# Starting expert weights a step earlier and reordering the handover from attention to experts

## The chip, the cores and the metric

The kernel runs on one core of a Trainium2 chip. The time is that of the device for one execution, in microseconds, as a median of timed runs. A profile of one execution is a separate run with its own span; positions in it are counted from the span's start. The engines are called PE (TensorE), DVE (VectorE), ACT (ScalarE), POOL (GpSimd) and SP (SyncE). A line number such as L446 is a line of the kernel before.

## The reference, cut to what matters

Two layers follow each other. The first is a gated linear attention (an mLSTM cell) over 4 batches of 8 heads, 768 steps and head size 40; its output, put together over the heads, gives 3072 rows of 320. The second is a mixture of 8 experts: a row goes to the one expert with the largest logit, through two matrices with a relu between, and is scaled by the softmax weight of that expert.

```python
def _attn_ref(q, k, v, i_gate, f_gate, o_gate):
    ...
    for t in range(S):
        m_new = np.maximum(f_gate[:, :, t] + m, i_gate[:, :, t])
        f_stab = np.exp(f_gate[:, :, t] + m - m_new)
        i_stab = np.exp(i_gate[:, :, t] - m_new)
        C = f_stab[..., None, None] * C + i_stab[..., None, None] * np.einsum('bhd,bhe->bhde', vt, kt)
        n = f_stab[..., None] * n + i_stab[..., None] * kt
        h_tilde = np.einsum('bhde,bhe->bhd', C, qt)
        denom = np.maximum(np.abs(nq), 1.0)          # nq = n . q
        y[:, :, t] = o * h_tilde / denom             # o = sigmoid(o_gate)

def _moe_ref(x, w_gate, w1, w2):
    logits = x @ w_gate
    expert_idx = np.argmax(logits, axis=1)
    ...
    for e in range(E):
        h = np.maximum(x_sorted[lo:hi] @ w1[e], 0.0)
        y_sorted[lo:hi] = h @ w2[e]
    return gate_w[:, None] * y_sorted[inv_perm]
```

## The kernel before

The attention runs in chunks of 128 rows, 24 in all, six to a batch. A loop over steps works on several chunks at once: step `s` makes the scores of chunk s+1, the transposes of s+2, the attention output of s, and the routing of older ones. Chunks are routed in teams of two: `logits`, `choose` (which expert), `gate` (softmax weight), `rank` and `place` (at which place of the expert's list). `keep_rows` scales the rows into bf16 and `send` scatters them on POOL into a sorted list in HBM. Each expert's list is then read back in tiles: tile (e, 0) has the first 256 places and holds only rows of chunks 0 to 15, tile (e, 1) the next 128. What is left over goes into extra tiles, whose weights are copied within SBUF once they are all there.

Each engine runs its instructions in the order in which they stand in the program, so that the place of a call in the source decides what it waits behind.

The weights of an expert are brought in by two functions. Both are DMAs that POOL issues[...]:

```python
    def weights_in(e, n=1):            # w1: three DMAs, 512 KB and twice 64 KB
        nc.gpsimd.dma_start(w1_all[:, e, : FL * F]..., bass.AP(moe_w1.tensor, ...))        # L181
        for i in range(2):
            nc.gpsimd.dma_start(w1_all[64 * i : 64 * i + 64, e, FL * F :], moe_w1[...])    # L186

    def weights_out(e0, n):            # w2: one DMA, 640 KB
        nc.gpsimd.dma_start(w2_all[:, e]..., moe_w2[e]...)                                 # L193
```

A tile is turned (transposed on PE, copied by DVE), goes through the first layer in pieces `u`, whose relu is DVE's for even and ACT's for odd pieces, and through the second layer, whose result ACT copies and POOL scatters to the output:

```python
    def turn(g):
        g["xT"] = spot("xT", [128, NP, n * 128], BF16)
        tp = spot("tp", [128, NP, n * 128], BF16)
        ... nc.tensor.transpose(tp[...], src[:, j, d0 : d0 + 128], ident_b[:])             # L242
        nc.vector.tensor_copy(g["xT"], tp)                                                 # L243

    def layer1(g, u):
        if u == 0: ...            # four banks "hp", the first matmuls of all pieces       # L260
        ... nc.tensor.matmul(hp[:, i, :], lhsT=w[...], rhs=xT[:, db, :], ...)              # L269
        if a == 0: nc.vector.tensor_relu(dst, hp)                                          # L275
        else:      nc.scalar.activation(dst, hp, AF.Relu)                                  # L277

    def layer2(g, j):
        zp = spot(g.get("zp", "zp"), [128, Dm], F32)
        ... nc.tensor.matmul(zp, lhsT=g["h"][...], rhs=g["w"][1][:, fb, :], ...)           # L282
        nc.scalar.copy(zo, zp)                                                             # L287
        nc.gpsimd.indirect_dma_start(out=out[:, :], ...)                                   # L289
        if j + 1 < g["n"]: pause()     # a memset on POOL, L299
```

The loop of steps, cut to what the change touches (NT is 24, PE_ is 7):

```python
        for s in range(-3, NT):
            P, odd = (s - 4) // 2, s % 2
            last = s == NT - 1
            do(scores, s + 1); do(transposes, s + 2); ...; do(values, s + 2)
            if odd and s > E and sent <= (...):
                send(sent); sent += 1
            if s == NT - 5:
                weights_in(0, 1)
            ...
            do(states, s); do(load, s + 6 if s >= -1 else -1)
            if pair: rank(P, s - 1)
            if last:
                warm(5)                # filler matmuls on PE, L569
            do(xtrans, s - 1)
            do(ogate, s + 2); do(attend, s)
            ...
            do(rows, s)                # x_sb and den on DVE, then x_sb on POOL (L446)
            if odd and 0 <= (s - 3) // 2:
                logits(...); choose(...); count(...)
            if s > E and sent <= upto:
                send(sent); sent += 1
            ...
            if s == 2 * PE_ + 5:
                for e in range(E):
                    receive(e, 0)
            if s == NT - 4: weights_out(0, 1)
            if s == NT - 3: weights_in(1, 1)
            if s == NT - 2: weights_out(1, 1)
        weights_in(2, 1)
        weights_out(2, 1)
```

What stands behind the loop is the tail: the routing of the last four chunks (team P0 with chunks 20 and 21, team P0 + 1 with 22 and 23) and the first two expert tiles, in buffers of the attention. Its order is in the diff below. The eight experts' remaining tiles follow, in the order (2,0), (3,0), (0,1), (1,1), (4,0), (2,1), (5,0), (3,1), (4,1), (6,0), (5,1), (7,0), (6,1), (7,1), and five extra tiles.

Of the kernel before, what the change touches and what calls it, by code (L numbers as in the profile page):

```python
# [9 lines left out]
BF16 = mybir.dt.bfloat16  # L10
# [9 lines left out]
def kernel(  # L20
# [153 lines left out]
    s_idx = rte.tile([128, E, NJ], I32)  # L174
    rest = rte.tile([128, 512], F32)
    zo_e = rte.tile([128, 4, Dm], F32)
    xg = [(x_all[:, NE * e : NE * (e + 1), :], x_all[:, NE * E + e : NE * E + e + 1, :]) for e in range(E)]

    def weights_in(e, n=1):
# [55 lines left out]
    def turn(g):  # L235
        n = g["n"]
        src = g["xg"] if "xg" in g else xg[g["e"]][g["k"]]
        g["xT"] = spot("xT", [128, NP, n * 128], BF16)
        tp = spot("tp", [128, NP, n * 128], BF16)
        for j in range(n):  # L240
            for a, d0 in enumerate(parts):
                nc.tensor.transpose(tp[:, a, j * 128 : (j + 1) * 128], src[:, j, d0 : d0 + 128], ident_b[:])  # L242
        nc.vector.tensor_copy(g["xT"], tp)  # L243
# [65 lines left out]
    with tc.tile_pool(name="ring", bufs=1) as ring_pool, \  # L309
# [295 lines left out]
            load(i)  # L605
        for i in range(1, NV):
            pads(i)
        sent = 0
        for s in range(-3, NT):
            P, odd = (s - 4) // 2, s % 2  # L610
            last = s == NT - 1
            do(scores, s + 1)
            do(transposes, s + 2)
            if s == -3:
                masks()
            if s == -2:
                gates()
                router()
            do(values, s + 2)
            if odd and s > E and sent <= (s - 5 if s > 2 * PE_ + 4 else s - 6):  # L620
                send(sent)
                sent += 1
            if s == NT - 5:
                weights_in(0, 1)
            pair = not odd and 0 <= P
            if pair:
                gate(P)
            do(states, s)
            do(load, s + 6 if s >= -1 else -1)
            if pair:  # L630
                rank(P, s - 1)
            if last:
                warm(5)
            do(xtrans, s - 1)
            do(ogate, s + 2)
            do(attend, s)
            if pair:
                place(P)
                if P == PE_:
                    even_out(s - 1)  # L640
            if s == 2 * PE_ + 4:
                keep_rows(s - 4)
                keep_rows(s - 3)
            elif s != 2 * PE_ + 5:
# [24 lines left out]
        assert sent == NT - 4  # L669
        early = [dict(e=e, n=NE, k=0, si=0, zp="hp") for e in range(2)]  # L670
        spots.update(
            hp=[(t_, ps1) for t_ in ("sA", "sB", "tk", "tq")], tp=[("dC", ps1)],
            h=[kq[:, i].rearrange("p a h d -> p (a h d)").bitcast(BF16) for i in range(2)],
            xT=[kq[:, 2, a].rearrange("p h d -> p (h d)").bitcast(BF16) for a in range(2)],
            zo=[zo_e[:, i, :] for i in range(4)],
        )
        for g in early:
            g["w"] = (w1_all[:, g["e"], :], w2_all[:, g["e"]])
        first, second = early
# [203 lines left out]
```

## Time and profile before

| | |
|---|---|
| time before, median of 3 runs | 218.2 us (218.13 to 219.56) |
| span of the profiled run | 208.9 us |
| granted TensorE clock, mean | 0.991 |
| PE busy | 184.8 us (88%) |
| PE weight load | 153.3 us (73%) |
| DVE busy | 125.7 us (60%) |
| ACT busy | 117.0 us (56%) |
| POOL busy | 137.7 us (66%) |
| DMA moved | 44.32 MB, mean 212 GB/s |

The chain that ended last consists of PE for 64%, of POOL for 9%, of DVE for 8%, of ACT for 6% and of DMA for 3%. Busy times are sums over the whole span and say little of a single stage: the attention loop ends near 118 us, the tail reaches to about 134, and the remaining expert tiles follow. A stage is read from windows and from the chain of waits within it. A line of the chain gives the start, the length and the instruction which the rest waited for at that time. The end of a DMA instruction on POOL in the timeline is not that of the transfer.

### The profile page before, as it was taken

The numbers are of one execution on the slowest core, as the hardware profiler recorded it, in microseconds if no ns is written. First come the engines' busy times: TensorE is split into PE (matmuls) and PEld (weight loads), VectorE is DVE, ScalarE is ACT, GpSimd is POOL, SyncE is SP. The second block draws the span as 40 slices with busy tenths as digits, with TensorE's granted clock in tenths as the row PEclk, the third lists the DMA queues.
The fourth block names the chain that finished last, engine by engine and source line by source line (L and its number), as shares of the span: only waits on it lengthen the run. The fifth ranks groups of instructions, "written<-read, shape, count | busy, mean of one in ns | idle before, by whom it ended". The sixth has DMA issues, their size and how long they took to land.

```text
span 208.9 us, 5733 instructions
## 1 busy us (share of the span) xinstructions
PE 184.8 (88%) x2051; PEld 153.3 (73%) x2060; DVE 125.7 (60%) x410; ACT 117.0 (56%) x273; POOL 137.7 (66%) x238
## 2 busy tenths in 40 slices
PE   2289999999999999998999898779999999999760
PEld 1176888888999999997788676557787777777540
DVE  7855656678787877978777644256684252534310
ACT  2458765888869978798584344224343343433320
POOL 6025779437477898784999948985437568885321
PEclk9999999999999999999999999999999999999996
DMA  7999999989999999999579999899999999999930
GB/s 135 192 193 197 198 245 197 215 175 204 197 205 175 176 173 197 189 204 175 92 140 187 265 239 209 131 206 255 240 227 221 225 250 270 399 391 382 365 123 24
DMA packets 116686, 44.32 MB, mean 212 GB/s; under 512 B 102506, under 2 KB 111725, under 8 KB 116656
## 3 DMA queue, kind: packets, MB, share of 16 engines
q1 hardware_dynamic: 105456, 25.34, 58.2%
q0 software_dynamic: 10736, 18.38, 40.0%
q8 instruction: 17, 0.28, 0.5%
q10 hardware_dynamic: 464, 0.21, 0.4%
q14 instruction: 13, 0.11, 0.1%
HBM read 39.30 MB, written 9.37 MB: 233 GB/s over the span
## 4 chain that ended last, share of the span: by engine, by line
PE 64%; POOL 9%; DVE 8%; issue 8%; ACT 6%; DMA 3%; POOLq 0%; ACTq 0%; DVEq 0%
PE zp L282 10%; PE hp L269 9%; PE hp L408 7%; PE hp L476 6%; PE tk L370 5%; PE dC L416 5%; PE tq L370 4%; PE xt L453 3%; PE sA L383 3%; PE sA L388 3%; DMA w_all<-in_moe_w_dram 3%; PE hp L260 3%; POOL out_dram L289 3%; POOL x_sorted L581 2%; PE tp L242 2%
## 5 line engine op out<-in xcount | busy, mean ns | idle before, releaser
L275 DVE TENSOR_SCALAR h<-hp 128x512 bf16<-128x512 f32 x25 | 17.3, 691 | 34.8 <-PE hp L269 16.1
L277 ACT ACTIVATE h<-hp 128x512 bf16<-128x512 f32 x25 | 14.9, 597 | 26.2 <-PE hp L269 24.8
L581 POOL DMA_INDIRECT x_sorted<-x_all,slots x24 | 25.2, 1050 | 5.8 <-issue 3.9
L446 POOL TENSOR_TENSOR x_sb<-x_sb,den 128x320 f32<-128x320 f32 x23 | 16.7, 727 | 17.4 <-DVE den L444 17.2
L289 POOL DMA_INDIRECT out_dram<-zo,s_idx x20 | 19.9, 995 | 9.7 <-DMA w_all<-in_moe_w_dram 4.8
L282 PE MATMUL zp<-w_all,h 128*128 128x320 bf16 x160 | 24.0, 299 | 0.0
L282 PEld LDWEIGHTS <-h 128*128 128x128 bf16 x200 | 18.8, 98 | 6.2
L395 ACT CAST dB<-sB 128x512 bf16<-128x512 f32 x24 | 14.0, 584 | 14.0 <-PE sB L389 12.7
L269 PEld LDWEIGHTS <-w_all 128*128 128x128 bf16 x256 | 19.0, 98 | 3.8 <-issue 1.1
L408 PE MATMUL hp<-C_sb,qT 104*128 104x82 f32 x160 | 20.6, 272 | 0.0
L287 ACT COPY zo<-zp 128x320 f32<-128x320 f32 x25 | 10.6, 425 | 17.7 <-PE zp L282 16.4
L370 PE MATMUL tk<-ident,kq 128*104 128x128 f32 x96 | 16.5, 297 | 4.1 <-DMA kq<-in_k_dram 4.1
L269 PE MATMUL hp<-xT,w_all 128*128 128x128 bf16 (+1 forms) x224 | 20.1, 243 | 0.0
L408 PEld LDWEIGHTS hp<-C_sb,qT 104*128 104x128 f32 x160 | 19.4, 192 | 0.3
L455 ACT COPY xT<-xt 128x384 f32<-128x384 f32 x24 | 11.6, 482 | 13.2 <-PE xt L453 12.9
L358 POOL CAST vAb<-vA 128x328 bf16<-128x328 f32 x24 | 11.0, 458 | 11.7 <-DVE vA L356 11.7
L396 POOL TENSOR_SCALAR_AFFINE_SELECT dB<-dB 128x512 bf16<-128x512 bf16 x24 | 16.5, 689 | 2.2 <-ACT dB L395 2.0
L416 PE MATMUL dC<-vA,kq 128*104 128x82 f32 x160 | 17.8, 254 | 0.0
L476 PE MATMUL hp<-wg_sb,xT 128*128 128x8 f32 x144 | 17.7, 256 | 0.0
L393 DVE TENSOR_TENSOR dA<-sA,cmask 128x512 bf16<-128x512 f32 x24 | 16.0, 668 | 1.9 <-PE sA L388 1.9
L476 PEld LDWEIGHTS hp<-wg_sb,xT 128*128 128x128 f32 x144 | 17.0, 192 | 0.0
L416 PEld LDWEIGHTS dC<-vA,kq 128*104 128x104 f32 x160 | 16.3, 172 | 0.0
(156 smaller groups left out, 450.5 us busy)
## 6 DMA issues: line engine op xcount, KB each, us to landing
wx<-w_all SPq DMA_DIRECT2D x10, 640.0 KB, 9.1
w_all<-in_moe_w_dram POOLq DMA_DIRECT2D x8, 640.0 KB, 11.1
w_all<-in_moe_w_dram POOLq DMA_DIRECT2D x8, 512.0 KB, 11.3
kq<-in_k_dram SPq DMA_DIRECT2D x24, 160.0 KB
kq<-in_q_dram SPq DMA_DIRECT2D x24, 160.0 KB
v<-in_v_dram SPq DMA_DIRECT2D x24, 160.0 KB, 3.9
o_sb<-in_o_gate_dram SPq DMA_DIRECT2D x24, 160.0 KB, 4.5
x_sorted<-zrow POOLq DMA_DIRECT2D x8, 241.5 KB, 3.4
```

The source lines that it names most:

```text
L269: nc.tensor.matmul(hp[:, i, :], lhsT=w[:, c : c + 255 : 2], rhs=xT[:, db, :], start=False, stop=(db == FL - 1), skip_group_check=True,)
L275: nc.vector.tensor_relu(dst, hp)
L282: nc.tensor.matmul(zp, lhsT=g["h"][:, fb, j * 128 : (j + 1) * 128], rhs=g["w"][1][:, fb, :], start=(fb == 0), stop=(fb == FB - 1),)
L289: ins = nc.gpsimd.indirect_dma_start(out=out[:, :], out_offset=bass.IndirectOffsetOnAxis(ap=at, axis=0), in_=zo, in_offset=None, bounds_ch ...
L370: nc.tensor.transpose(tp[:, j, :], two(d[n], j), ident[:])
L393: nc.vector.tensor_tensor(d["dA"][:], sA[:], cmask[:, None, :].to_broadcast([128, PR, 128]), op=ALU.mult)
L396: nc.gpsimd.affine_select(d["dB"][:], d["dB"][:], compare_op=ALU.is_ge, fill=0.0, base=0, pattern=[[0, PR], [1, 128]], channel_multiplier=-1,)
L408: nc.tensor.matmul(hp[:, 2 * j * D1 : (2 * j + 2) * D1], lhsT=d["qT"][:, j, :], rhs=st["C"][:, j].rearrange("p h d -> p (h d)"), start=(j ...
L416: nc.tensor.matmul(st["dC"][:, j], lhsT=two(d["k"], j), rhs=d["vA"][:, 2 * j : 2 * j + 2, :], start=(c == 0 and j == 0), stop=True, skip_g ...
L446: eng.tensor_tensor(x3d, x3d, den[:].unsqueeze(2).to_broadcast([128, H, D]), op=ALU.mult)
L476: nc.tensor.matmul(lg[:, i * E : (i + 1) * E], lhsT=st[t]["xT"][:, db * 128 : (db + 1) * 128], rhs=wg_sb[:, db, :], start=(fresh and i == ...
L581: ins = nc.gpsimd.indirect_dma_start(out=xs[:, :], out_offset=bass.IndirectOffsetOnAxis(ap=slots[:, t : t + 1], axis=0), in_=x_all[:, t, : ...
```

## The change

The change has five parts.

- The weights of the first experts start one step earlier: w1 of expert 0 in step 18 (NT - 6) rather than 19, and each of the following moved up by one place, so that w1 of expert 2 is issued at the end of step 22.
- The first expert tile is turned inside the last step, in the place of five filler matmuls, so that its copy stands ahead of DVE's work on the last chunk. Its first layer then begins the tail.
- The routing of the last chunks is spread between the pieces of the first tile's layers, with the gate, rank and sends of the first pair ahead of the logits of the last pair.
- The second tile is turned before the last rank; the second layers of the two early tiles write into the two PSUM banks "hp" of the pool `ps2`, which the attention output used, rather than into those of the first layer.
- The third tile (2, 0) is turned in the tail, into an SBUF buffer of its own, before the second tile's second layer.

```diff
+    xT_2 = rte.tile([128, NP, NE * 128], BF16)
...
-        g["xT"] = spot("xT", [128, NP, n * 128], BF16)
-        tp = spot("tp", [128, NP, n * 128], BF16)
+        g["xT"] = g["xT"] if "xT" in g else spot("xT", [128, NP, n * 128], BF16)
+        if "tp" in g:
+            tag, pool = g["tp"]
+            tp = pool.tile([128, NP, n * 128], BF16, name="tp", tag=tag)[:]
+        else:
+            tp = spot("tp", [128, NP, n * 128], BF16)
...
+        early = [dict(e=e, n=NE, k=0, si=0, zp="zp") for e in range(2)]
+        spots.update(
+            hp=[(t_, ps1) for t_ in ("sA", "sB", "tk", "tq")], tp=[("dC", ps1)], zp=[("hp", ps2)],
...
+        third = dict(e=2, n=NE, k=0, si=0, xT=xT_2[:], tp=("xt", ps1))
...
-            if s == NT - 5:
+            if s == NT - 6:
                 weights_in(0, 1)
...
             if last:
-                warm(5)
+                targets(0, 0)
+                turn(first)
+                warm(3)
             do(xtrans, s - 1)
...
+            if s == NT - 5:
+                weights_out(0, 1)
             if s == NT - 4:
-                weights_out(0, 1)
+                weights_in(1, 1)
             if s == NT - 3:
-                weights_in(1, 1)
+                weights_out(1, 1)
             if s == NT - 2:
-                weights_out(1, 1)
-        weights_in(2, 1)
+                weights_in(2, 1)
         weights_out(2, 1)
-        early = [dict(e=e, n=NE, k=0, si=0, zp="hp") for e in range(2)]
...
-        targets(0, 0)
-        turn(first)
-        warm(3)
+        layer1(first, 0)
         xtrans(NT - 1)
-        layer1(first, 0)
-        logits(P0 + 1, NT)
         gate(P0)
         rank(P0, NT - 1)
+        layer1(first, 1)
         place(P0)
-        layer1(first, 1)
         for t in (NT - 4, NT - 3):
             keep_rows(t)
             send(t)
             pause()
+        logits(P0 + 1, NT)
         choose(P0 + 1)
+        layer1(first, 2)
         gate(P0 + 1)
-        layer1(first, 2)
-        layer1(first, 3)
+        targets(1, 0)
+        turn(second)
         rank(P0 + 1, NT, 2 * E)
         place(P0 + 1)
+        layer1(first, 3)
         for t in (NT - 2, NT - 1):
             keep_rows(t)
             send(t)
             pause()
         nc.vector.tensor_copy(tot[:], rt[P0 + 1]["tot"])
         weights_in(3, 1)
         weights_out(3, 1)
-        targets(1, 0)
-        turn(second)
         layer2(first, 0)
         layer2(first, 1)
         for u in range(4):
             layer1(second, u)
+        targets(2, 0)
+        turn(third)
         weights_in(4, 1)
         weights_out(4, 1)
         layer2(second, 0)
         layer2(second, 1)
...
-    ready(groups[0])
+    groups[0]["xT"] = third["xT"]
```

More of the change, by code (lines that the diff above doesn't have):

```diff
@@ L607 @@
             pads(i)
+        early = [dict(e=e, n=NE, k=0, si=0, zp="zp") for e in range(2)]
+        spots.update(
+            hp=[(t_, ps1) for t_ in ("sA", "sB", "tk", "tq")], tp=[("dC", ps1)], zp=[("hp", ps2)],
+            h=[kq[:, i].rearrange("p a h d -> p (a h d)").bitcast(BF16) for i in range(2)],
+            xT=[kq[:, 2, a].rearrange("p h d -> p (h d)").bitcast(BF16) for a in range(2)],
+            zo=[zo_e[:, i, :] for i in range(4)],
+        )
+        third = dict(e=2, n=NE, k=0, si=0, xT=xT_2[:], tp=("xt", ps1))
+        for g in (*early, third):
+            g["w"] = (w1_all[:, g["e"], :], w2_all[:, g["e"]])
+        first, second = early
         sent = 0
@@ L660 @@
                     receive(e, 0)
+            if s == NT - 5:
+                weights_out(0, 1)
             if s == NT - 4:
-                weights_out(0, 1)
+                weights_in(1, 1)
             if s == NT - 3:
-                weights_in(1, 1)
+                weights_out(1, 1)
             if s == NT - 2:
-                weights_out(1, 1)
-        weights_in(2, 1)
+                weights_in(2, 1)
         weights_out(2, 1)
         assert sent == NT - 4
-        early = [dict(e=e, n=NE, k=0, si=0, zp="hp") for e in range(2)]
[L671 to L679, printed above, removed]
-        targets(0, 0)
-        turn(first)
-        warm(3)
+        layer1(first, 0)
         xtrans(NT - 1)
-        layer1(first, 0)
-        logits(P0 + 1, NT)
         gate(P0)
         rank(P0, NT - 1)
+        layer1(first, 1)
         place(P0)
-        layer1(first, 1)
         for t in (NT - 4, NT - 3):
```

## The prediction

> **What bounds the kernel now.** I read the page first. PE is busy for 88% of the span, which would say "TensorE-bound". But busy time is an average over stages, so I next asked for a table of two-microsecond windows, then for the chain of waits around the handover from attention to experts. The windows (us from the span's start; busy us of PE, PE weight load, DVE, ACT and POOL with instruction counts; granted clock; DMA share; GB/s):
>
> ```profile
> 98.00:100.00 2.00, 2.00 (x26) 1.96 (x26) 1.63 (x6) 0.85 (x2) 1.93 (x3) 1.00 0.83 159
> 100.00:102.00 2.00, 1.95 (x21) 1.38 (x20) 1.77 (x8) 0.86 (x2) 1.83 (x4) 1.00 0.10 32
> 108.00:110.00 2.00, 2.00 (x27) 1.99 (x26) 1.39 (x5) 1.23 (x3) 1.99 (x4) 1.00 0.46 116
> ...
> 124.00:126.00 2.00, 1.06 (x17) 0.72 (x17) 0.92 (x4) 2.00 (x9) 1.58 (x3) 1.00 1.14 226
> ...
> 132.00:134.00 2.00, 1.66 (x17) 1.19 (x15) 0.20 (x1) 0.85 (x2) 1.78 (x3) 1.00 0.75 63
> 138.00:140.00 2.00, 1.05 (x11) 0.61 (x12) 0.28 (x1) 0.00 (x0) 1.58 (x3) 1.00 1.17 216
> 140.00:142.00 2.00, 1.98 (x21) 1.57 (x19) 1.40 (x3) 0.87 (x2) 1.59 (x2) 1.00 1.19 243
> ...
> 178.00:180.00 2.00, 2.00 (x21) 1.56 (x18) 1.46 (x4) 1.14 (x2) 1.44 (x2) 1.00 0.97 391
> ```
>
> Two things are to be seen. The DMA engines run dry when the last chunk has been loaded (100 to 102) and again before the weights of expert 3 move (132 to 134), while from 136 to 198 their share is 1.0 to 1.2 in every window. And PE has real holes only between 118 and 140; after 140 it is full until 196. So after 140 PE and DMA are both saturated, and the whole rest hangs on when that stage starts. What starts it, in the chain of waits (start, us, what):
>
> ```profile
> 101.38 0.78 POOL w_all L181
> 102.15 1.12 POOL w_all L186 x2
> 103.27 0.75 POOL x_sb L446
> ...
> 123.56 1.00 ACT x_all L575 x2
> 124.56 0.57 ACT gex L515 x4
> ...
> 129.66 0.97 POOL x_sorted L581
> 130.64 0.54 POOL rest L299
> 131.18 0.70 POOL w_all L181
> 131.88 0.52 POOL w_all L186
> 132.40 6.78 DMA w_all<-in_moe_w_dram
> 139.18 0.05 issue
> 139.23 0.61 PE hp L260 x7
> ```
>
> The last four chunks' rows leave one after the other on POOL (124.40 to 131.1, four times send plus pause, 1.75 us each by their starts 124.40, 126.19, 127.94, 129.66). Only behind them does POOL issue the weights of expert 3, and tile (3,0) waits for these until 139.2. From there the end follows at a fixed distance.
>
> **What the Trainium skill says.** "Perfetto Trace Analysis", section "DMA Instruction — SWDGE (GPSIMD)": the profiler ends such an instruction when the descriptors are written, not when the data is there. The trace agrees: the issue of the 512 KB of w1 takes 0.78 us on POOL, its landing 11.3 us. "DMA: Bandwidth & Descriptors", section "Issuing engines are not separate DMA queues": transfers of SP and of POOL share the 16 engines, so weights that start earlier compete with the last loads; here share 1.07 at 96 to 98, with no weights yet. The same page, "Anatomy of one DMA — SWDGE (gpsimd) path", fits 2.0 us plus bytes over 436 GB/s per DMA, 3.5 us for 640 KB; this trace is slower, 5.6 us for the first expert's w1 into nearly idle DMA engines (issued 101.38; the windows' GB/s add up to 640 KB near 107) and about 8 us for expert 3's. The measured ones are used. "TensorE: Matmul & The Clock Gate", section "What's actually happening": an idle window of about 3.4 us halves the clock. Before, the clock is 1.00 in every window up to 204, and no hole is that long.
>
> **The change part by part.** Single times are from the timeline of 94 to 146 us.
>
> *Weights one step earlier.* Step 18's POOL work leaves a hole of 2.44 us, between the cast of vA (ends 94.69) and x_sb (97.13, waiting for DVE's den). The issue of one w1 takes 0.78 + 1.15 = 1.95 us and fits in it: POOL pays nothing, and the data starts moving at about 97 instead of 103. In step 19 the w1 issue at 101.38 to 103.2 disappears from in front of x_sb, which the transposition at 104.08 waited for: PE's idle 0.41 us there goes. The later issues I place by adding POOL's durations (affine_select 0.65, cast 0.46, x_sb 0.73, tick and send 1.25, w1 1.95, w2 0.80): w2 of 0 at 103.3 (was 108.34), w1 of 1 at 107.4 (112.17), w2 of 1 at 112.4 (116.84), w1 of 2 at 116.4 (118.96), w2 of 2 at 119.8 (121.86). Worth to the end by itself: only the 0.4 us, since expert 3's issue is not among them. It clears the DMA queue and POOL for what follows.
>
> *First tile turned inside step 23.* Before, the copy of the turned tile stands in DVE's order behind the rows and the choice of step 23, and ends at 120.06; PE waits 0.90 us for it. After, it is done near 115.5, in a stretch in which DVE is idle (114.8 to 116.5). Five fillers (1.24 us at 114.66) go; the eight transposes (0.45) and three fillers (0.64) take their place, before a transposition that waited for x_sb anyway. So layer one starts behind the logits of step 23, at 117.2 (117.6 less 0.4) instead of 120.1.
>
> *Routing ahead of the layers.* Before, PE did the logits of team 11 (1.4 us) and layer pieces in such an order that ACT stood on the relu of piece 1 until 123.07, and the rows of chunks 20 and 21 (ACT, 123.56) behind it. After: layer piece 0 until 118.3, xtrans 118.7, rank of team 10 at 118.9 (behind DVE's choice), piece 1 until 119.4. ACT: xT copy until 119.3, four gate steps (4 x 0.245) until 120.2, relu 0.6 until 120.8, two row copies of 0.5: the first is done at 121.3. Its send can start at 121.4 instead of 124.40, if POOL is through with w2 of expert 2 by then (120.6). The pair 22, 23: logits of 11 until 120.8, choice until about 121.9, gate until 122.9, relu of piece 3 and rows until 123.9, slots at 124.3 behind the second tile's copy on DVE; POOL asks for them at 121.4 + 2 x 1.75 = 124.9. So they do not hold it up. Four sends end at 121.4 + 4 x 1.75 = 128.4, and expert 3's weights are issued there: 131.1 - 128.4 = **2.7 us earlier**.
>
> *PSUM and the third tile.* Layer two writes into the two banks of the attention output instead of rotating through those of layer one, and the third tile is turned before layer two of the second. This removes the wait for its copy (0.97 us at 134.6). Counting PE on: piece 3 ends at 122.8, two layer twos (2 x 2.17), layer one of the second 2.5, transposes 0.45 and layer one of the third 2.5 end near 132.6 (was 137.5), perhaps half a us later for the bank that still holds the last ranks. PE then stands before tile (3,0) until its weights land: 128.4 + 8.1 = 136.5. Of PE's own gain of nearly 5 us, 2.2 are turned into a longer wait.
>
> *Sum.* Tile (3,0) starts at 136.5 instead of 139.2. Behind it DMA has the same weights 4 to 7, the same receives and the same five copies of weights for the extra tiles, all at a share of 1.0 or more, and the same PE work. The end moves by 2.7 us: 218.2 - 2.7 = 215.5. I take 215.4, as less queued ahead of expert 3 may save a little more in its landing.
>
> **Rivals.**
>
> *The weights land sooner.* With experts 0 to 2 fetched early, expert 3 may land in the 5.6 us of the first one instead of 8.1. PE would then be its own limit, near 134, and the gain up to 5 us: 213.3. Against it: the next experts still leave POOL only 2.7 us earlier, POOL stands on their transfers (2.67 and 3.04 us, at 152.57 and 157.47), and DMA is full from 136 on.
>
> *The gain is given back.* If DMA alone sets the end (36 us of transfers for 4 to 7, then the copies at about 390 GB/s until 199), and its holes merely move to 124 to 130 while POOL is sending, the end would move by less than the weights' issue: one us, 217.2.
>
> *New waits in steps 18 to 23.* The tile for the early turn may not have landed (received from 108.30 on, landing at least 6.8 us later, so 115.1; the receive itself moves up by nearly 2 us with the send of chunk 15, but the DMA is fuller); PE in order would stand up to 1 us. The last loads, issued until 98.3, share DMA with the first weights; the last keys are needed at 105.7, so there are some 3 us of slack. POOL may stop in w1 of expert 2 for earlier weights, as it did for 1.10 us at 121.33. Together at worst 2 to 3 us, and then the time stays at 218.
>
> *A cold PE.* The wait before (3,0) grows to some 3.5 us. If that halves the clock, the next matmuls lose about 2 us: 217.5. DMA would hide part.
>
> **Range and chances.** The centre is the 2.7 us of the send chain. Against me by 2.4 us (a late receive plus a POOL stop) gives 217.8; in favour by 2.2 us (sooner landing) gives 213.2. Two per cent is 4.4 us, which needs the first rival nearly in full: 0.16. For slower by as much I see no mechanism large enough: 0.04. Within 2%: 0.80. I assume that what the profiled span gains the timed run gains too.
>
> **What would show it.** In the changed profile: the first w1 issue near 94.7 to 97 and no low DMA window at 100 to 102; the first tile's copy before DVE's rows of step 23; the send of chunk 20 near 121.4 and expert 3's w1 issue near 128.4; PE idle some 3 us before tile (3,0), at a start near 136.5; a last stretch of unchanged length. I am wrong if expert 3's issue has not moved, if the early turn waits for its receive, if POOL stands on earlier weights inside the send chain, or if tile (3,0) moved by 2.7 us and the end did not, which would mean that DMA's total and not the start of that stage sets the end.

## The result and the profile after

The changed kernel takes 213.2 us (median of 4 runs, 210.2 to 214.9) where the kernel before takes 218.8 (218.1 to 219.6): a ratio of 0.966, with an interval of 0.955 to 0.977. Here and below, medians and ranges are of all runs, while a ratio leaves out the slow ones, those more than 1.5% above the fastest run of their kernel. Predicted were 215.4 us and a range of 213.2 to 217.8. The gain is 5.6 us instead of 2.8.

In the profile after, lines of code have moved: L186, L260, L299 and L581 of before are L187, L265, L304 and L586 now. The table of two-microsecond windows (us; busy us of PE, PE weight load, DVE, ACT and POOL; granted clock; DMA share; GB/s):

```profile
98.00:100.00 2.00, 2.00 (x25) 1.87 (x25) 1.58 (x7) 0.85 (x2) 1.98 (x3) 1.00 1.04 178
100.00:102.00 2.00, 1.95 (x21) 1.47 (x21) 1.83 (x8) 0.99 (x3) 1.80 (x4) 1.00 1.24 214
108.00:110.00 2.00, 1.95 (x23) 1.61 (x20) 1.52 (x7) 1.30 (x3) 2.00 (x5) 1.00 1.15 248
124.00:126.00 2.00, 2.00 (x22) 1.34 (x20) 0.16 (x1) 0.76 (x3) 1.71 (x5) 1.00 1.18 211
132.00:134.00 2.00, 0.57 (x10) 0.40 (x7) 1.19 (x3) 0.60 (x1) 1.82 (x3) 1.00 1.13 191
138.00:140.00 2.00, 2.00 (x13) 1.25 (x12) 1.34 (x5) 0.50 (x1) 0.00 (x0) 0.64 1.10 304
140.00:142.00 2.00, 2.00 (x28) 1.44 (x27) 0.00 (x0) 0.85 (x2) 1.33 (x2) 1.00 1.11 219
178.00:180.00 2.00, 2.00 (x13) 1.50 (x12) 0.79 (x3) 0.76 (x2) 1.70 (x3) 0.50 0.96 374
```

The hole of DMA at 100 to 102 is filled (share 1.24 instead of 0.10), and PE is full at 124 to 126. What is left of PE's holes stands at 132 to 134: 0.57 us of work, then a wait. New are two stretches at half the clock, one behind that wait and one near 178. The chain of waits through the handover (start, us, what):

```profile
123.02 1.00 ACT x_all L580 x2
124.02 0.33 ACT zo_e L292
124.42 0.96 issue
125.37 0.54 POOL rest L304
126.12 0.98 POOL x_sorted L586
127.10 0.54 POOL rest L304
127.64 0.70 POOL w_all L182
128.34 0.51 POOL w_all L187
128.88 5.64 DMA w_all<-in_moe_w_dram
134.56 0.61 PE hp L265 x7
```

It is the chain of before: rows, sends, the issue of expert 3's weights, their landing, tile (3,0). Only everything lies earlier. Issue: 127.6 instead of 131.1. From issue to the tile: 6.7 us instead of 7.8. Start of the tile, as PE's own timeline has it (start, us, [wait before it]):

```profile
113.97 0.61 PE L247 MATMUL tp<-ident_b,x_all 128*128 128x128 bf16 x8
117.01 0.61 PE L265 MATMUL hp<-kq,w_all 64*128 64x256 bf16 x8
126.95 0.61 PE L247 MATMUL tp<-ident_b,x_all 128*128 128x128 bf16 x8
134.22 0.95 PE L265 MATMUL hp<-xT,w_all 64*128 64x256 bf16 x8 [1.64 <-DMA w_all<-in_moe_w_dram]
```

and the last of these in the kernel before:

```profile
138.86 0.97 PE L260 MATMUL hp<-xT,w_all 64*128 64x256 bf16 x8 [1.31 <-DMA w_all<-in_moe_w_dram]
```

The first four are the first tile turned, its layer one, the third tile turned, and tile (3,0) at 134.2, which was 138.9 in the profile before: 4.6 us earlier. Yet the profiled span shrank only from 208.9 to 208.5. The experiments had to explain both: why 4.6 and not 2.7, and where 4.2 us of the profile went.

### The profile page after: what moved, and what is told of

The parts are those of the page before. It is cut to its first block, busy times and chain, and to the rows that moved or that the text cites. A ratio compares the mean times of both kernels' runs of the same rounds, so it can differ in the third digit from the quotient of the medians.

```text
span 208.5 us, 5724 instructions
## 1 busy us (share of the span) xinstructions
PE 186.1 (89%) x2046; PEld 154.6 (74%) x2055; DVE 126.1 (61%) x410; ACT 117.1 (56%) x273; POOL 137.9 (66%) x238
## 4 chain that ended last, share of the span: by engine, by line
PE 59%; issue 10%; DVE 10%; POOL 8%; DMA 7%; ACT 4%; POOLq 0%; DVEq 0%; ACTq 0%
PE hp L413 8%; PE hp L481 7%; PE zp L287 7%; PE hp L274 6%; PE dC L421 5%; PE tk L375 5%; DMA out_dram<-zo,s_idx 5%; POOL out_dram L294 5%; PE tq L375 4%; PE sA L388 4%; PE xt L458 3%; PE sA L393 3%; DMA w_all<-in_moe_w_dram 3%; PE hp L433 2%; PE hp L265 2%
## 5 line engine op out<-in xcount | busy, mean ns | idle before, releaser
L586 POOL DMA_INDIRECT x_sorted<-x_all,slots x24 | 25.5, 1061 | 4.9 <-issue 3.1
L287 PE MATMUL zp<-w_all,h 128*128 128x320 bf16 x160 | 24.9, 306 | 0.0
L287 PEld LDWEIGHTS <-h 128*128 128x128 bf16 x200 | 19.3, 100 | 6.7
L274 PEld LDWEIGHTS <-w_all 128*128 128x128 bf16 x256 | 19.8, 102 | 4.6 <-issue 1.3
L274 PE MATMUL hp<-xT,w_all 128*128 128x128 bf16 (+1 forms) x224 | 22.2, 256 | 0.0
```

The lines of the kernel that those rows point to most:

```text
L274: nc.tensor.matmul(hp[:, i, :], lhsT=w[:, c : c + 255 : 2], rhs=xT[:, db, :], start=False, stop=(db == FL - 1), skip_group_check=True,)
L287: nc.tensor.matmul(zp, lhsT=g["h"][:, fb, j * 128 : (j + 1) * 128], rhs=g["w"][1][:, fb, :], start=(fb == 0), stop=(fb == FB - 1),)
L586: ins = nc.gpsimd.indirect_dma_start(out=xs[:, :], out_offset=bass.IndirectOffsetOnAxis(ap=slots[:, t : t + 1], axis=0), in_=x_all[:, t, : ...
```

## The experiments

Each group of runs had its own runs of the kernel before; ratios are to those.

**Both kernels again, and each half of the change.** `weights only` is the kernel before with the six weight issues one step earlier; `tail only` is the changed kernel with them where they were.

```
-            if s == NT - 5:          # weights only, in the kernel before
+            if s == NT - 6:
                 weights_in(0, 1)     # and so on for the other five
```

> The kernel before, once more. Its profiled span was 208.9 us and its timed runs 218.1 to 219.6, nearly 8 us above the usual distance of 1.8 us. Theory S (the start of the saturated stage sets the end): the timed runs are the profiled one plus a constant of the timing, so 218 +- 1 again, ratio 1.00, clock near 0.99. Theory H (holes: the usual execution of before has a hole of several us and a halved TensorE clock in the saturated stage, which the shown profile happened to lack): a new profile has a span near 216 with a clock below 0.98, or the runs fall on two levels, 210 and 218.

> The changed kernel, once more. Both theories: a ratio between 0.955 and 0.977 to the kernel before. Theory S: expert 3's tile starts 4 to 5 us earlier than before in every profile (134.5 against 139.2) and the end follows but for what a slower clock takes. Theory H: the profile has the same early start, yet its end relative to the start of that tile differs from run to run by several us (74.0 in the shown profile, 69.7 in that of before).

> Only the weights are moved up by one step; the last step and the tail are those of the kernel before. My working gives this part 0.4 us: ratio 0.995 to 1.000, expert 3's w1 issued near 130.7 and tile (3,0) started near 138.5. Rival (the early start of the transfers is what counts, as DMA's total sets the end): 3 to 6 us, ratio 0.97 to 0.985, although expert 3's issue hardly moves.

> All of the change but the early weights: these stay at steps 19 to 23. By my working the order of the tail is what moves expert 3's issue: near 128.5 to 129.5, 2 to 2.5 us before that of the kernel before, ratio 0.983 to 0.990. Rival (DMA's total): hardly any gain, ratio 0.995 to 1.005, because the holes of the DMA engines at 100 to 110 us stay.

| run | us, median (range) | ratio (interval) | send of chunk 20 | issue of w1 of 3 | tile (3,0) | end of span |
|---|---|---|---|---|---|---|
| before again | 217.5 (215.9–218.6) | 0.999 (0.996–1.002) | 124.9 | 131.9 | 139.5 | 216.9 |
| weights only | 215.9 (212.9–216.2) | 0.985 (0.974–0.995) | 123.5 | 130.2 | 137.5 | 214.3 |
| tail only | 215.1 (214.5–215.8) | 0.987 (0.981–0.994) | 123.5 | 130.7 | 139.4 | 213.7 |
| changed again | 212.6 (210.4–214.7) | 0.973 (0.963–0.984) | 121.4 | 128.1 | 134.4 | 210.2 |

Each half brings the issue forward by 1.2 to 1.7 us, both together by 3.8. But the profiles are shifted against each other before the first changed instruction runs: ACT's copy of xT for chunk 17, ahead of all the weights, starts at 94.8 in the kernel before, at 93.9 with the weights alone and at 94.6 in the other two. The copies for chunks 18 and 19 follow, in the kernel before and, below, with the weights alone:

```profile
99.06 0.48 ACT L455 COPY xT<-xt 128x384 f32<-128x384 f32 x1 [0.62 <-PE dC L416]
105.19 0.48 ACT L455 COPY xT<-xt 128x384 f32<-128x384 f32 x1 [0.85 <-PE xt L453]
98.23 0.48 ACT L455 COPY xT<-xt 128x384 f32<-128x384 f32 x1 [0.61 <-PE dC L416]
103.79 0.48 ACT L455 COPY xT<-xt 128x384 f32<-128x384 f32 x1 [0.34 <-PE xt L453]
```

Counted from the copy for chunk 17, the send of chunk 20 comes 0.6 us earlier with the weights alone, 1.3 with the tail alone and 3.4 with both; tile (3,0) comes 1.2, 0.1 and 5.0 us earlier. Two engines hold the first send, and neither half alone frees both. With the weights alone ACT still holds the rows (timeline of ACT):

```profile
119.23 0.19 ACT L515 ACTIVATION_READ_ACCUMULATOR gex<-lgs,lmin 128x1 f32 x1
122.20 0.60 ACT L277 ACTIVATE kq<-hp 128x512 bf16<-128x512 f32 x1 [2.78 <-PE hp L269]
122.70 1.00 ACT L575 ACTIVATE x_all<-x_sb,gsum 128x320 bf16<-128x320 f32 x2
```

ACT stands 2.78 us on layer one's piece before it may scale the rows. With the tail alone the rows are ready, but POOL is not (timeline of POOL):

```profile
119.36 0.74 POOL L182 DMA_DIRECT2D w_all<-in_moe_w_dram  x1
120.10 0.56 POOL L187 DMA_DIRECT2D w_all<-in_moe_w_dram  x1
121.63 0.52 POOL L187 DMA_DIRECT2D w_all<-in_moe_w_dram  x1 [0.97 <-DMA w_all<-in_moe_w_dram]
122.19 0.77 POOL L194 DMA_DIRECT2D w_all<-in_moe_w_dram  x1
123.51 1.03 POOL L586 DMA_INDIRECT x_sorted<-x_all,slots  x1 [0.47 <-DMA x_sorted<-x_all,slots]
```

Expert 2's weights are issued at 119.4 to 123.0, in front of the send. The early weights are thus no extra of 0.4 us: without them the reordered tail runs into POOL.

The end does not follow tile (3,0) in every row, though. PE's timeline with the tail alone has these two waits, at tile (3,0) and at tile (7,0):

```profile
139.35 1.36 PE L265 MATMUL hp<-xT,w_all 64*128 64x256 bf16 x8 [5.70 <-DMA w_all<-in_moe_w_dram]
181.23 0.65 PE L265 MATMUL hp<-xT,w_all 64*128 64x256 bf16 x8 [2.37 <-DVE xT L248]
```

Tile (3,0) starts only 0.2 us earlier than in the kernel before run again, though its weights were issued 1.2 us earlier. Behind the wait of 5.7 us the granted clock is 0.50 from 138 to 144, and the next tile starts at 146.6 instead of 145.0. Yet the span is 3.2 us shorter. That is won at the second wait, a hole of 2.4 us here and 6.8 us in the kernel before (shown below), and in the half clock behind it. So the gain of the tail alone is not shown to come from its earlier send.

**Do the copies of weights at the end limit it?** From about 175 on, five experts' weights are copied for the extra tiles (L790 and L791 before). Three ways to change that: use experts 0 to 4 in place without a copy (the extra tiles then compute with other experts' weights), address the right expert's weights by a register of PE, and use two buffers for the copies instead of four.

```
-        groups[len(order) + x]["w"] = fetch(expert_of(x))
+        groups[len(order) + x]["w"] = (w1_all[:, x, :], w2_all[:, x])                      # no copies
+        ex = nc.tensor.value_load(xe[0:1, x : x + 1], ...)                                 # direct
+        ... w1_all[:, bass.ds(ex, 1), :], w2_all[:, bass.ds(ex, 1)], copying only the 64-row part
-XW = 4
+XW = 2                                                                                     # two buffers
```

> The kernel before without the ten copies of weights for the five extra tiles: these tiles use the weights of experts 0 to 4 in place, so their rows of the output are not the reference's. Theory S+H (the start of the saturated stage counts, and the usual hole of 6 to 9 us at tile (7,0) belongs to the copies): the hole on DVE and ACT and the halved clock at 184 to 192 us are gone, the time falls by 7 to 12 us, to 206 to 211. Rival (the hole has to do with the weights of expert 7 or with something else): the hole stays, and the time falls by 3 us at most.

> The changed kernel without the copies, in the same way. Theory S+H: no hole, and against the kernel before without copies the whole earlier start of tile (3,0) is left: 4.5 to 5.5 us, so 201 to 206. Rival (the gain lies in the hole at tile (7,0), which the change shortens): the two kernels without copies lie within 2 us of each other.

> The changed kernel with the extra tiles' matmuls reading the expert's weights in place by a register of PE; only the 64-row part of w1 (128 KB each) is still copied, so 0.64 MB instead of 6.4 MB. It computes the whole result. If the copies make the hole and set the end of the stage: 203 to 208 us. If reading a register on PE costs more than 1 us each: 208 to 212.

> The changed kernel with two buffers for the copies instead of four: the first copy is issued two tiles later, at most two experts' copies are in flight. If the hole is a matter of how many copies are queued: it shrinks, and the time is 0 to 3 us lower, less what the later start of the copies costs. If a single copy makes it: the hole comes later and the end with it, 213 to 217 us.

Beside 217.2 us (215.2 to 218.8) for the kernel before: without copies 215.6 (ratio 0.995, 0.987 to 1.002) before and 212.5 (0.982, 0.975 to 0.990) after, with starts of tile (3,0) at 138.5 and 135.4. The kernels lie 3.1 us apart, where I had expected 4.5 to 5.5. The starts lie 3.1 us apart, or 4.1 counted from the copy of xT for chunk 17, so that the gain is roughly that of the start. Where the hole described next is there, the copies do not limit either kernel. In profiles without it PE does wait for a copy near the end, for 1.9 us in the kernel before and 3.2 us in the changed kernel of the fourth group. Direct addressing costs 227.0 us (1.047, 1.040 to 1.054), two buffers 220.9 (1.019, 1.011 to 1.026; PE waits 4.9 us for a late copy at 203): both worse.

**A hole near tile (7,0).** In most profiles of these two groups PE, DVE and ACT stand still once, near 172 to 188. In the kernel before, run again, PE's timeline has this line:

```profile
187.77 0.61 PE L260 MATMUL hp<-xT,w_all 64*128 64x128 bf16 x8 [6.78 <-DVE xT L243]
```

PE waits for DVE's copy of a turned tile, and DVE's timeline has:

```profile
185.07 0.69 DVE L275 TENSOR_SCALAR h<-hp 128x512 bf16<-128x512 f32 x1 [9.22 <-remote]
```

ACT's, of the same run:

```profile
186.90 1.08 ACT L277 ACTIVATE h<-hp 128x512 bf16<-128x512 f32 x2 [7.44 <-remote]
```

"remote" means that the trace doesn't show who released them. PE's records have the matmuls of (7,0) at 177.2, but DVE gets the first results only at 185.1 and ACT its own at 186.9. The profile that the prediction rests on has no such hole: it ran once in 210.7 us, while the kernel's three timed runs took 218. The profile after has a short one (2.7 us of PE, the half clock near 178 above). The hole stays without the copies. Two more guesses were the run of output scatters on POOL and PE's instruction stream (see `quiet rows` and `fillers` below).

**Moving only the issue of expert 3's weights.** Later by five pauses in the changed kernel (`late w3`), or in front of the last two of the four sends, in the changed kernel and in the kernel before (`early w3`); and the changed kernel without the output rows of six groups (`quiet rows`).

```
+        for _ in range(5):             # late w3
+            pause()
         weights_in(3, 1)
         weights_out(3, 1)
```

```
+        weights_in(3, 1)               # early w3; the same two lines go below
+        weights_out(3, 1)
         for t in (NT - 2, NT - 1):
             keep_rows(t)
             send(t)
             pause()
```

> The changed kernel with five more pauses of POOL (0.53 us each, about 2.7 us) ahead of the issue of expert 3's weights; nothing else differs. If the end hangs on the start of tile (3,0), the issue goes from 127.6-128.1 to about 130.5, and tile (3,0) starts near 136.5-137 (landing 6.0 to 6.6 us, as in the changed kernel): the time rises by 2 to 2.7 us, to about 215. If instead the sum of the transfers behind it sets the end, it rises by less than 1 us. For the landing: if it is short in the changed kernel because less is queued ahead of the weights, it stays at 6.6 us or gets shorter here; if it is only the hour of the issue that counts (a landing of 7.6 to 7.8 us for an issue near 131), tile (3,0) starts past 138.

> The changed kernel with expert 3's weights issued between the second and the third of the last four sends instead of behind the fourth. Issue near 124.4 instead of 127.6-128.1; landing 6.3 to 6.6 us, so the weights are there near 131, and the bound of tile (3,0) becomes PE's own work, near 132.5 (2 us earlier than 134.4). The last two sends move 2.7 us later, past 130; tile (0,1), the first that needs them, is due near 136 and should not wait. If the start of the saturated stage sets the end: 1.5 to 2 us faster than the changed kernel, about 211. If the transfers behind it are the limit by now: within 0.7 us of the changed kernel. If the late sends hold up tile (0,1): as slow as the changed kernel or slower, with a wait before (0,1) in the records.

> The kernel before with the same one edit: expert 3's weights issued between the second and the third of the last four sends. Issue near 127.9 instead of 131.1-131.9. If the hour of that issue is the whole of what the change does, and the landing is 6.3 to 7.8 us, the weights are there by 135.7, but PE arrives at tile (3,0) only at 137.5 (as with the early weights alone): start at 137.5 instead of 139.2, gain about 1.7 us, time 216. If landing alone counted and PE were ahead, the gain would be 3 us or more. If POOL's later sends hold up the second parts, less than 1 us.

> The changed kernel without the output rows of the fifth to the tenth group of expert tiles: their layer two and its copy stay, only POOL's scatters of the rows into the output are left out (so those rows of the output are missing). These are the scatters that POOL sends in one run near 171 to 182, behind the weights of expert 7. If that run of scatters is what makes the hole of PE, DVE and ACT near tile (7,0) (6 us in most profiles), the hole goes: the time falls by 4 to 6 us, to about 208, and the granted clock has no halved stretch there. If the hole has another cause (PE's instructions, the weights of expert 7), it stays at its place and the time falls by less than 1.5 us.

In this group the kernel before took 212.2 us (210.3 to 214.2), five less than in the groups so far. `late w3` took 209.8 (209.1 to 219.5; 0.989, 0.979 to 0.999), `early w3` 218.6 (211.1 to 224.3), the kernel before with early w3 214.9 (1.015, 1.004 to 1.026), `quiet rows` 212.6 (209.6 to 221.9; 0.996, 0.992 to 1.000). The third is clear: with the sends behind the weights, tile (3,0) started at 138.5, but the next tile then stood on the second part of its rows. PE's timeline of it:

```profile
145.76 0.61 PE L242 MATMUL tp<-ident_b,x_all 128*128 128x128 bf16 x4 [4.83 <-DMA x_all<-x_sorted]
```

The changed kernel with early w3 has the same wait, of 6.25 us. The four sends cannot be passed over: (0,1) needs them. I had expected no wait there. The other runs said little alone, since the changed kernel was not in the group. So it was run again in the next group, the fourth, with late w3 and quiet rows, and with 64 small matmuls (`fillers`) in PE's wait before tile (3,0):

```
+        j = ps1.tile([128, 512], F32, name="junk", tag="tk")
+        for _ in range(64):
+            nc.tensor.matmul(j[:, :16], lhsT=ident_b[:], rhs=ident_b[:, :16], start=True, stop=True)
```

> The changed kernel again, as the measure for the other three of this group, since on the chip of the last group the kernel before took 212.2 us and not 217 to 218, without the hole of PE near tile (7,0). If the gain is the earlier start of tile (3,0) (4.7 to 5.1 us), it is 5 us on any chip: 212.5 where the kernel before takes 217.5, 207.5 where it takes 212.2. If part of the gain is that the hole costs the changed kernel less, the gain is about 2 us where the kernel before has no hole (210).

> Expert 3's weights issued 2.7 us later than in the changed kernel, as in the run before, this time beside the changed kernel on the same chip. If the end hangs on the start of tile (3,0): 2 to 2.7 us slower than the changed kernel. If the transfers behind it, or a hole of a fixed hour, set the end: less than 1 us slower.

> The changed kernel with 64 small matmuls of PE (128x16) behind the second tile's layer two, while PE waits for expert 3's weights: about 2 to 4 us of PE time, at most 2 us of it past the arrival of the weights. They move everything behind them by 128 instructions of PE and keep its clock up before tile (3,0). If the hole near tile (7,0) comes from PE's own instruction fetch (which lies at its start in every profile with a hole), it moves to another tile or goes. If it belongs to the tile (weights of expert 7) or to POOL's run of scatters, it stays before tile (7,0) or (6,1). The time: within 1.5 us of the changed kernel if the hole stays; up to 5 us faster if it goes.

> The changed kernel without the output rows of the fifth to the tenth group, again: on the chip of the last group even the kernel before showed no hole, so that the run told nothing. On a chip where the changed kernel has the hole near (7,0): if the run of scatters makes it, it is gone here and the last tile starts 4 to 6 us earlier than in the changed kernel; if not, it stays.

The kernel before took 211.7 us again (210.8 to 214.9). The changed kernel took 208.6, 213.4, 214.8 and 216.0 in its four runs; late w3 211.7 (210.6 to 222.4; 1.000, 0.996 to 1.004); fillers 208.1 (207.3 to 208.7; 0.982, 0.976 to 0.987); quiet rows 219.8 (213.8 to 222.2). So the changed kernel can be slower than the kernel before here. Its best run is 3.1 us below the kernel before, between the 2 and the 5 us that I had put for a kernel without the hole, and 3 us below late w3, as it should be if the start of tile (3,0) sets the end; but that is one run, and the other three lie above late w3. The profile, of the run of 213.4 us, shows what held that one up: DVE stands 5.1 us until 112.2, PE 2.4 us until 114.1, and the clock is 0.50 from 116 to 120. The waits of 100 to 122 name the load of the last values (us in total, times, longest):

```profile
DVE vA L361 <- DMA v<-in_v_dram: 6.5, 2, 5.1
```

and SP's timeline shows how it came late:

```profile
95.78 2.54 SPq L350 DMA_DIRECT2D o_sb<-in_o_gate_dram  x1
98.37 3.62 SPq L350 DMA_DIRECT2D kq<-in_k_dram  x1
102.04 0.84 SPq L350 DMA_DIRECT2D kq<-in_q_dram  x1
102.98 0.79 SPq L350 DMA_DIRECT2D v<-in_v_dram  x1
103.86 1.01 SPq L350 DMA_DIRECT2D o_sb<-in_o_gate_dram  x1
```

POOL issues expert 0's w1 at 94.1. The issues of loads that follow take 2.5 and 3.6 us instead of 0.8. When SP is so far that only the last one to three loads are still to come, it costs nothing; when the whole last chunk is, its loads go out at 96 to 105 and an engine waits 5 to 8 us for one of them. Of the thirteen profiles with both parts of the change and w1 issued at 94 to 95.4, four have the chunk still to come (this one, late w3 and early w3 of the group before, quiet rows here). These four, of runs of 213.4 to 224.3 us, are the ones with such a wait.

**The weights behind the loads.** If so, issuing the first weights at the end of step 18 has to stop it:

```
-            if s == NT - 6:            # was in front of the gates of step 18
-                weights_in(0, 1)
+            if s == NT - 6:            # now its last instruction on POOL
+                weights_in(0, 1)
```

> The changed kernel with the 64 small matmuls before tile (3,0), again, with more repetitions, beside the next one. Where the kernel before takes 211.7 to 212.2 us: 208 when nothing is late, and some executions of 213 to 222 in which the last loads of step 18 (values or output gate) come 3 to 8 us late, because the weights of expert 0 stand in the DMA queues beside them, if that is what spread the changed kernel over 208.6 to 216 us. Where the kernel before takes 217 to 218 (hole near tile (7,0)): 208 if the hole moves or goes with the 128 added instructions, 212.5 to 213.5 if it stays.

> The same with the first weights' issue at the end of step 18 (about 99 us) instead of in the middle of it (94.5), behind the last loads (issued until 98.3). If the early weights are what makes the last loads late: no execution above 212 where the kernel before takes 212, and the PE hole near 112 us never comes; the price is at most 0.5 us (x_sb of step 19 behind the issue, as in the kernel before), so about 208 to 208.5. If the late loads have another cause, the spread stays as in the run beside it.

Kernel before 212.0 us (210.7 to 214.5), fillers 207.6 (207.1 to 208.3; 0.979, 0.974 to 0.984), guarded 209.8 (207.8 to 212.0 in 22 runs; 0.987, 0.984 to 0.990). SP's last load with fillers, from its timeline:

```profile
95.99 3.47 SPq L350 DMA_DIRECT2D o_sb<-in_o_gate_dram  x1
```

The same load in the guarded kernel:

```profile
96.20 0.92 SPq L350 DMA_DIRECT2D o_sb<-in_o_gate_dram  x1
```

The long issue is gone, 0.9 us instead of 3.5. In all six profiles with w1 issued at 99 or later, this load takes 0.5 to 1.8 us to issue, so the early weights make the long one. That they also make the spread of the times is not shown. None of the 22 guarded runs is above 212.1, but none of the ten runs with fillers was disturbed either, though their w1 is issued at 94 to 95 and I had expected some at 213 to 222; the fillers come after step 23, and why SP was further on in them is open. The price of guarding is 2.2 us and not 0.5: w1 is issued at 99.5 instead of 94.1, and layer one of the first tile starts 24.3 us behind the copy of xT for chunk 17 instead of 22.9. Fillers is the fastest version by its median, but level with the best run of the changed kernel beside it (208.6); it was never in a group in which the kernel before takes 218.

## Why the prediction was right or wrong

**What limits it: right up to tile (7,0).** Sends, issue of expert 3's weights, tile (3,0), then a stage of fixed length. From the last start of tile (3,0) behind its weights to the end of the span there are, in the profiles without a hole near (7,0) that keep all their output rows and their late sends, 70.0 us (before, 138.9 to 208.9), 70.8 (changed, 140.8 to 211.6), 70.4 and 70.5 (late w3, 147.4 to 217.8 and 139.1 to 209.6), 69.1 and 69.4 (fillers, 137.4 to 206.5 and 135.9 to 205.3) and 69.5 (guarded, 138.0 to 207.5). The starts lie 11.5 us apart, the distances less than 2. A stretch of PE's work within it is more constant still. From the first matmul of tile (0,1) to that of tile (7,0) it is, in the kernel before,

```profile
144.21 0.40 PE L260 MATMUL hp<-xT,w_all 64*128 64x128 bf16 x8
176.42 0.61 PE L260 MATMUL hp<-xT,w_all 64*128 64x256 bf16 x8
```

and in the changed kernel run again

```profile
139.59 0.40 PE L265 MATMUL hp<-xT,w_all 64*128 64x128 bf16 x8
171.80 0.61 PE L265 MATMUL hp<-xT,w_all 64*128 64x256 bf16 x8
```

32.2 us both times, and so in 13 of the 20 profiles, for starts of tile (0,1) from 139.6 to 159.7. The rival "the gain is given back", with DMA's total as the limit, falls with that up to tile (7,0). Behind it, every profile with all output rows and a start of tile (3,0) before 135.9 has a hole, so that there the fixed length is not shown for the starts at 134.2 and 134.4 of the changed kernel. And the tail alone (above) gained its time behind tile (7,0), not by an earlier tile (3,0).

**Single steps.** POOL's issues came at 103.5, 107.5, 112.4, 116.1 and 119.3 (predicted 103.3, 107.4, 112.4, 116.4, 119.8); x_sb was not delayed; layer one of the first tile started at 117.0 (117.2); the turned copy was through before DVE's rows; the third tile was turned before layer two of the second.

**Where it failed: "Tile (3,0) starts at 136.5 instead of 139.2".** It started at 134.2 and 134.4. Of the 2.3 us missing in the profile after, 0.8 are the issue (127.56 instead of 128.4). The send of chunk 20, which I had at 121.4, came at 120.84, and four sends take 6.7 us to the issue and not 4 x 1.75 = 7.0; they took 6.7 in the kernel before as well (124.40 to 131.10). The other 1.4 are the landing: 6.66 us from the issue to the tile's first matmul, where I had 8.1. Of these, 0.3 are my reading: 139.23 in the chain is a later group of the tile's matmuls, the first came at 138.86, 7.8 us behind the issue. So 1.1 us are a landing that really was shorter. That is the rival "the weights land sooner", on which the 0.16 for faster rested; it came about half true.

Why they landed sooner stays open. Neither the hour of the issue nor what is queued ahead of it settles it. PE's timelines of the changed kernel in the fourth group and of fillers in the last have

```profile
140.75 0.61 PE L265 MATMUL hp<-xT,w_all 64*128 64x256 bf16 x7 [0.28 <-DMA w_all<-in_moe_w_dram]
135.93 0.61 PE L265 MATMUL hp<-xT,w_all 64*128 64x256 bf16 x7 [0.97 <-DMA w_all<-in_moe_w_dram]
```

The first was issued at 134.16 and landed in 6.6 us, the second at 127.36, nearly the hour of the profile after, and landed in 8.6. Late w3 took 7.8 us (issued at 131.35), two buffers 8.0 (128.52).

**"Worth to the end by itself: only the 0.4 us": about right for the step it names.** From the copy of xT for chunk 18 to that for chunk 19 the kernel before takes 6.1 us and the kernel with the weights alone 5.6, and with the weights alone the send of chunk 20 moves by just these 0.6 us. The time fell by more, 2.0 us (217.9 to 215.9, by the interval of the ratio 1.0 to 5.6); where the rest comes from is not shown. What the part left out is its worth to the other one: it takes the issue of expert 2's weights out of the way of the send which the tail brings forward, so that the two give 3.4 us at the send and not 0.6 + 1.3. (0.78 + 1.15 in that part is 1.93 and not 1.95, which changes nothing.)

**"I assume that what the profiled span gains the timed run gains too": wrong.** The span went from 208.9 to 208.5, the time from 218.8 to 213.2. The profile of before was one without the hole near (7,0), the timed runs were of the length with it. In the profile after, tile (0,1) and tile (7,0) start at

```profile
141.02 0.40 PE L265 MATMUL hp<-xT,w_all 64*128 64x128 bf16 x8
176.01 0.61 PE L265 MATMUL hp<-xT,w_all 64*128 64x256 bf16 x8 [2.72 <-DVE xT L248]
```

Of the 4.6 us gained at tile (3,0), 3.2 are left at tile (0,1), as the half clock makes tile (3,0) 1.4 us longer, and 0.4 at tile (7,0), behind the hole. With the hole the same distance is 77.4 us (before again), 75.8 (changed again), 74.3 (the profile after), so 4 to 7 us more, in both kernels. Between the two repeated kernels, 5.1 us of the 6.7 by which the spans differ are the start of (3,0) and 1.6 are a shorter rest.

**Rivals.** "New waits in steps 18 to 23" I had put at 2 to 3 us at worst, with "some 3 us of slack" for the last loads. In four profiles it is 5 to 8 us. Where the kernel before takes 212, three of the changed kernel's four runs are slower than that, and the profiled one of them has this wait. "A cold PE" came as well: half the clock from 136.0 to 139.4 in the profile after, where the 16 matmuls of layer one of (3,0) took 2.76 us instead of 1.92. The Trainium skill, "TensorE: Matmul & The Clock Gate", section "What's actually happening", has the clock halve after at least one idle window of some 3.4 us; here PE had been idle for only 1.64 us, and at work throughout the window from 130 to 132. In the changed kernel run again 1.35 us of idling left the clock at 1.00, and so did 1.97 us without the copies and 2.26 us with direct addressing. So the length of the wait alone does not decide it.

**Left open.** What makes the hole near (7,0), and why whole groups of runs have it and others not. It is not the copies (it stays without them), and not simply the chip: the first group of experiments and the last both ran on chip 0, and the kernel before took 217.9 and 212.0 us there. In the two groups in which the scatters were left out and PE's instructions shifted, no profile has the hole, so these tell nothing of it. One packet of the DMA queue for instructions lies close to the start of tile (7,0) where there is a hole (177.0 to 177.5 in the kernel before again), but also where there is none (175.5 to 176.0 in the profile before), so it alone does not make it.

## What to carry to other kernels

When two engines hold the same instruction, neither fix alone shows what it is worth: size the pair by the instruction that both release (here the send, 0.6 and 1.3 us alone and 3.4 together), and not part by part. Count from an instruction that the change cannot have touched: here the profiles were up to 1.3 us apart by then. To see what an earlier start is worth, look for a stretch behind it whose length does not depend on when it starts (here 32.2 us), and for what lies behind that stretch. A transfer moved into a hole of one queue can stop the issue of small loads on another: ask how much of these is still to be issued at that moment, and what is late if all of it is. And before taking a profile as the base, compare its own run's time with the timed runs: here they were 7.5 us apart (210.7 and 218.2), and the repeated profile showed a stall that the first didn't have.

## What was not expected of the hardware

- The kernel before has two levels, by group of runs: medians of 217.2 to 218.8 us in three groups and 211.7 to 212.2 in three. In the repeated profile of the first kind DVE gets results at 185.1 whose matmuls PE's records begin at 177.2.
- With 640 KB of weights issued on POOL's queue, one or two of SP's following load issues took 2.0 to 5.0 us each instead of about 0.8, where loads were still to be issued some 2 us after the weights; in two profiles (weights only, direct) the last load was out before or took 1.4 us.
- The kernel whose extra tiles address their weights by a register took 227.0 us beside 217.2 for the kernel before, although it saves most of the copies. Sixteen first-layer matmuls of an extra tile took 1.9 to 3.4 us in it instead of 1.07, in part at half the clock.
- 64 small matmuls in a wait of PE made the changed kernel no slower: 207.3 to 208.7 us beside its best run of 208.6.
